# Reordering the head of a fused Fourier-mixing and expert kernel: which transfer stands ahead of which

## The chip, the cores and the metric

The kernel runs on one core of one Trainium2 chip. The metric is device time in microseconds (us) for one execution of the whole program. The kernel before was timed in three runs: 1634.4, 1637.09 and 1637.64 us, median 1637.09. A profiled execution of it took 1631.37 us, with a span of 1629.8 us in the trace; all times below that are given as positions ("at 201.6") are us from the start of that span.

## The reference

Two steps follow one another. The first mixes each sequence by a filter in the frequency domain, the second sends each of the resulting rows through one of eight small two-layer networks, chosen by a hash of the token number.

```python
# x: (8, 2496, 256) float32; filt_r, filt_i: (1249, 256)
X = np.fft.rfft(x, axis=1)
y = np.fft.irfft(X * (filt_r + 1j * filt_i)[None], n=2496, axis=1)   # (8, 2496, 256)

rows = y.reshape(19968, 256)
expert = token_ids * 2654435761 % 8                                # one of 8 per row
for e in range(8):                                                 # w1: (8, 256, 1024), w2: (8, 1024, 256)
    m = expert == e
    out[m] = np.maximum(rows[m] @ w1[e], 0.0) @ w2[e]
```

## The kernel before

The Fourier transform over 2496 = 39 x 64 points is done as three stages of matmuls per batch, with DRAM in between because each stage wants the data in another layout:

- **Stage 1** (six units per batch, tile `pa`): loads x in three parts (`load1`, v = 0, 1, 2), multiplies by `wf_t`, ScalarE copies the result out of PSUM and stores it to `d1` in DRAM.
- **Stage 2** (eleven units, tiles `pb`, `pc`): loads `t2` from `d1` in five parts (`load2`), multiplies by the table `d_t`; VectorE multiplies by the filter `f_t`; TensorE multiplies by the transposed table `e_t`; ScalarE copies the result and stores it to `d2`.
- **Stage 3** (six units, tile `pd`): loads `t4` from `d2` in three parts (`load4`), multiplies by `wi_t`, ScalarE copies into one of two buffers `o`, and GpSimd scatters the rows of `o`, up to four scatters for each unit, to their sorted places in `xs`.

The expert part then runs over 163 tiles of 128 sorted rows: load a tile `xg` from `xs`, transpose, two matmuls with a ReLU in between, scatter the rows to the output. The expert part can begin when batches 0 and 1 are through all three stages. What comes ahead of it is called the head here. The stages of batches 2 to 7 are woven into the expert tiles.

The order in which the head is emitted is given by hand: each piece has a number (its place in time), and the list is sorted by it. Every engine then works through its own instructions in that order, and the queues of SyncE, ScalarE and GpSimd issue their DMAs in that order. The numbers are places, not microseconds.

```python
    def load1(self, v):                      # x, in 3 DMAs on SyncE's queue
        k = self.b * NV + v
        if k < 4:                            # the first four parts lie in the weights' buffers
            xt = ws[k // 2][k % 2][0:NR]
            ...
        else:
            xt = xpool.tile([NR, XL, C], F32, ...)          # 2 buffers
        for h in range(H):
            nc.sync.dma_start(out=xt[h:NR:H, 0:n, :], in_=...)

    def load2(self, g):                      # t2: 4 buffers, 2 DMAs each on SyncE's queue
        ...
    def load4(self, v):                      # t4: 2 buffers, SyncE's queue
        ...
    def stage3(self, u):
        o = opool.tile([NR, XG, W], F32, ...)               # 2 buffers
        ...                                                 # VectorE writes the row numbers into o (line 288)
        self.products(wi_t, ..., o, copy, u, "pd")          # matmuls and copies
        for i in range(n):
            scatter(o[0:r, i, :], sidx[0:r, self.b, j:j + 1], f"xs_{self.b}")   # GpSimd

    def weights(i, which):                   # for i < 2: GpSimd's queue, 1 MB each
        eng = nc.gpsimd if i < 2 else nc.sync
        ...

    nc.sync.dma_start(out=wf_t[:], in_=wf_dram.ap())
    for v in range(NV):
        batches[0].load1(v)                  # x of batch 0
    ...
    S_PARTS = (slice(0, 8), slice(8, NS))    # tables and filters in two parts, NS = 20
    def load_tables(part):                   # d_t and both filters: GpSimd's queue, two DMAs on ScalarE's
        ...
    def spread_filters(part):                # sign and copy to the other 64 partitions
        ...
    def way_back(k):                         # e_t[4k:4k+4] from d_t by four transposes
        ...
    def count(): ...                         # VectorE and two small matmuls: rows of each expert
    def route(): ...                         # VectorE: the sorted place of each row
    def places():                            # the places to DRAM and back as indices sidx
        ...
        nc.gpsimd.dma_start(out=slot_dram[:]..., in_=slot_i[:])
        load_tables(1)
        ...                                  # three loads of sidx
    def blanks(): ...                        # seven scatters of empty rows into xs
```

Of the kernel before, what the change touches and what calls it, by code (L numbers as in the profile page):

```python
# [11 lines left out]
F32 = mybir.dt.float32  # L12
# [17 lines left out]
NS, NQ = N1 // 2 + 1, 64  # L30
# [6 lines left out]
NU = (HN + XG) // XG  # L37
# [75 lines left out]
def kernel(  # L113
# [10 lines left out]
    nc = tc.nc  # L124
# [3 lines left out]
    d_dram = nc.inline_tensor(d_host, name="d_tbl")  # L128
# [5 lines left out]
    def pool(stack, name, bufs, space=None):  # L134
        kw = {} if space is None else {"space": space}
        return stack.enter_context(tc.tile_pool(name=name, bufs=bufs, **kw))
# [23 lines left out]
    d_t = cpool.tile([P, NS, P], F32)  # L160
# [147 lines left out]
    batches = [Batch(b) for b in range(B)]  # L308
# [5 lines left out]
    def weights(i, which):  # L314

        if i >= NT:
            return
        if i >= 2 and which == 0:
            ws[i] = ws[i - 2]
        eng, kw = nc.gpsimd if i < 2 else nc.sync, {}  # L320
        e = eng.value_load(chunk_i[0:1, 0, i:i + 1], min_val=0, max_val=E - 1)
        if i >= 2:
            kw = {"cond": eng.value_load(chunk_i[0:1, 1, i:i + 1], min_val=0, max_val=1)}
        if which == 0:
            eng.dma_start(out=ws[i][0][:], in_=moe_w1[bass.ds(e, 1)].rearrange("one (dp p) f -> p (one dp) f", p=P), **kw)
        else:
            eng.dma_start(out=ws[i][1][:], in_=moe_w2[bass.ds(e, 1)].rearrange("one (fp p) d -> p (one fp) d", p=P), **kw)
# [3 lines left out]
    rpool = pool(rctx, "route", 1)  # L331
# [7 lines left out]
    nc.scalar.dma_start(out=rt[:], in_=r_dram.ap())  # L339
    nc.vector.tensor_copy(tokno[:], rt[0:NR, G + 2 + NQP:])  # L340

    S_PARTS = (slice(0, 8), slice(8, NS))

    def load_tables(part):
        sl = S_PARTS[part]
        nc.gpsimd.dma_start(out=d_t[:, sl, :], in_=d_dram.ap()[:, sl, :])
        for k in range(2):
            load_filter(k, sl)

    def load_filter(k, sl):  # L350
        filt = (filt_r, filt_i)[k]
        for q in range(2):
            off, step = (0, C) if q == 0 else (N1 * C, -C)
            (nc.gpsimd if k or sl.start else nc.scalar).dma_start(
                out=f_t[k][64 - 64 * k + 32 * q:96 - 64 * k + 32 * q, sl, :],
                in_=bass.AP(tensor=filt.tensor, offset=filt.offset + off + sl.start * step,
                            ap=[[N1 * C, 32], [step, sl.stop - sl.start], [1, C]]))

    def spread_filters(part):
        sl = S_PARTS[part]  # L360
        nc.vector.tensor_scalar(f_t[0][0:64, sl], f_t[0][64:128, sl], -1.0, None, op0=OP.mult)
        nc.scalar.copy(f_t[1][64:128, sl], f_t[1][0:64, sl])

    def way_back(k):

        ps = fps.tile([P, 4, P], F32, name=f"pe_{k}", tag="f")
        for i in range(4):
            nc.tensor.transpose(out=ps[:, i, :], in_=d_t[:, 4 * k + i, :], identity=ident[:])
        sl = slice(4 * k, 4 * k + 4)
        nc.scalar.activation(out=e_t[:, sl, :], in_=ps[:], func=AF.Identity, scale=sign[:])  # L370
# [102 lines left out]
    def places():  # L473
        slot, slot_i = rv["eid"], rv["eid_i"]
        nc.vector.tensor_reduce(slot[:], rv["acc"][:].rearrange("p e j -> p j e"), axis=AX.X, op=OP.add)
        nc.vector.tensor_copy(slot_i[:], slot[:])
        nc.gpsimd.dma_start(out=slot_dram[:].rearrange("(p j) -> p j", p=P), in_=slot_i[:])
        load_tables(1)
        for h in range(H):
            n = HN + (h == 0)  # L480
            slots = slot_dram[:]
            nc.gpsimd.dma_start(out=sidx[N1 * h:N1 * h + N1, :, 0:n],
                                in_=bass.AP(tensor=slots.tensor, offset=slots.offset + H0[h],
                                            ap=[[N2, N1], [S, B], [1, n]]))
# [62 lines left out]
    def spaced(t0, t1, n):  # L547
        return [t0 + (t1 - t0) * u / n for u in range(n)]

    def part1(b, at, loads=None):  # L550
        bt = batches[b]
        if loads is None:
            loads = [at[2 * v] - 2.5 * (at[1] - at[0]) for v in range(NV)]
        return ([(at[u], lambda u=u: bt.stage1(u)) for u in range(NU)] +
                [(loads[v], lambda v=v: bt.load1(v)) for v in range(NV) if b > 0])

    def part2(b, at, ready):
        bt = batches[b]
        return ([(at[u], lambda u=u: bt.stage2(u)) for u in range(NS // 2 + 1)] +
                [(max(at[2 * g] - 4.5 * (at[1] - at[0]), ready), lambda g=g: bt.load2(g)) for g in range(NS // SG)])  # L560

    def part3(b, at, ready):
        bt = batches[b]
        return ([(at[u], lambda u=u: bt.stage3(u)) for u in range(NU)] +
                [(max(at[2 * v] - 2.5 * (at[1] - at[0]), ready), lambda v=v: bt.load4(v)) for v in range(NV)])
# [4 lines left out]
    N_2 = NS // 2 + 1  # L570

    todo = part1(0, spaced(-153, -143, NU)) + [(-152.5, count), (-152.4, route)]
    todo += [(-154, lambda: load_tables(0)), (-129.5, places)]
    todo += [(t, lambda k=k: way_back(k)) for k, t in enumerate([-142.7, -142.5, -119.5, -119, -118.5])]
    todo += [(-129, lambda: spread_filters(0)), (-118.3, lambda: spread_filters(1))]
    todo += part2(0, spaced(-128, -95, N_2), -142)
    todo += part1(1, spaced(-123.5, -105, NU), [-141.5, -135, -134.5])
    todo += [(-125, tile_experts), (-121, experts), (-108, blanks)]  # L580
    todo += [(-110, lambda: nc.sync.dma_start(out=wi_t[:], in_=wi_dram.ap()))]
    todo += [(-118.2 + .1 * i, lambda i=i: (weights(i, 0), weights(i, 1))) for i in range(2)]
    todo += part2(1, spaced(-94, -60, N_2), -103) + part3(0, spaced(-84, -51, NU), -94.5)
    todo += part3(1, spaced(-54, -21, NU), -62) + part1(2, spaced(-52, -19, NU), [-85, -80, -41])

    todo += part1(3, spaced(2, 7, NU)) + part1(4, spaced(15, 20.5, NU))
    todo += part1(5, spaced(21, 27, NU)) + part1(6, spaced(36, 46, NU)) + part1(7, spaced(50, 60, NU))
# [109 lines left out]
```

## Time and profile before

The span splits into a head and the rest. From 207 on TensorE is almost always busy; up to 207 it is so for little more than half of the time.

| stretch (us) | what runs | TensorE busy (us) | granted clock | DMA share | GB/s |
|---|---|---|---|---|---|
| 0 to 42 | stage 1 of batch 0, tables, routing | 16.77 | 0.92 | 0.71 | 191 |
| 42 to 97 | stage 2 of batch 0, stage 1 of batch 1 | 38.32 | 0.81 | 0.97 | 308 |
| 97 to 148 | stage 2 of batch 1, stage 3 of batch 0 | 35.43 | 0.83 | 0.86 | 267 |
| 148 to 184 | stage 3 of batch 1, stage 1 of batch 2 | 24.55 | 0.83 | 0.70 | 203 |
| 184 to 207 | the turn to the expert part | 9.19 | 0.57 | 0.70 | 221 |
| 207 to 1630 | experts, batches 2 to 7 | 1394.54 | 1.00 | 0.47 | 146 |

How to read it: the busy time is how long the engine had an instruction at work in that stretch; the granted clock is the TensorE clock as a share of its full speed; the DMA share is the mean busy share of the core's 16 DMA engines. The queues are called q1 (SyncE), q10 (ScalarE) and q0 (GpSimd).

### The profile page before, as it was taken

How to read it: one execution, taken by the hardware profiler on the slowest of the kernel's cores; microseconds unless marked ns; L12 is line 12 of the kernel's file. 1: busy time of each engine (PE TensorE's matmuls, PEld its weight loads, DVE VectorE, ACT ScalarE, POOL GpSimd, SP SyncE). 2: the span in 40 equal slices, each digit the busy share in tenths (PEclk: the TensorE clock that was granted, in tenths of full speed). 3: DMA queues.
4: the chain of work that ended last, by engine and by line, in shares of the span. 5: the costliest groups of instructions: out<-in, count | busy, mean ns of one | idle time of the engine just before them, and what ended most of it. 6: DMA issues, size and time to landing. Idle time of an engine off the chain costs nothing.

```text
span 1629.8 us, 26685 instructions
## 1 busy us (share of the span) xinstructions
PE 1518.8 (93%) x9522; PEld 1381.7 (85%) x9522; DVE 539.0 (33%) x1022; ACT 217.1 (13%) x371; POOL 355.7 (22%) x375
## 2 busy tenths in 40 slices
PE   3676589999999999999999999999999999999997
PEld 2554378988888999899989998999999999999997
DVE  6572142452244444233434442222122121221221
ACT  2322212112111111111111111000000000000000
POOL 0235300331320132122121322233111111111111
PEclk9788699999999999999999999999999999999999
DMA  7998627747864883674537643544152413132220
GB/s 189 306 290 244 198 98 205 240 165 207 245 218 150 244 256 111 194 197 147 185 114 222 199 135 115 147 127 162 45 203 79 140 37 126 52 94 88 84 84 9
DMA packets 152541, 258.77 MB, mean 159 GB/s; under 512 B 16185, under 2 KB 118508, under 8 KB 150410
## 3 DMA queue, kind: packets, MB, share of 16 engines
q1 hardware_dynamic: 103345, 163.46, 33.1%
q0 software_dynamic: 21136, 50.96, 9.4%
q10 hardware_dynamic: 27928, 42.65, 8.3%
q8 instruction: 76, 1.25, 0.3%
q14 instruction: 56, 0.45, 0.1%
HBM read 431.87 MB, written 86.09 MB: 318 GB/s over the span
## 4 chain that ended last, share of the span: by engine, by line
PE 42%; issue 36%; POOL 7%; DMA 3%; DVE 2%; POOLq 1%; ACT 0%; SPq 0%; ACTq 0%; DVEq 0%
PE ups L630 15%; PE dps L642 15%; POOL out_dram L646 6%; PE pb L240 3%; PE pa L203 3%; PE pc L263 3%; PE pd L203 2%; POOL xs L301 2%; DMA xs<-o,sidx 1%; PE xps L619 1%; DVE z L250 1%; PE pa L198 0%; POOLq L646 0%; DMA d<-g 0%; DVE y L247 0%
## 5 line engine op out<-in xcount | busy, mean ns | idle before, releaser
L630 PEld LDWEIGHTS ups<-xt,w 128*128 128x128 f32 x5216 | 610.3, 193 | 9.2 <-DVE xt L621 1.0
L630 PE MATMUL ups<-xt,w 128*128 128x128 f32 x5216 | 611.1, 276 | 0.6 <-DVE xt L621 0.6
L642 PE MATMUL dps<-w,ht 128*128 128x256 f32 x2608 | 591.0, 380 | 0.0
L642 PEld LDWEIGHTS dps<-w,ht 128*128 128x128 f32 x2608 | 490.0, 191 | 63.7 <-issue 1.6
L646 POOL DMA_INDIRECT out_dram<-osb,xg x163 | 159.6, 979 | 944.6 <-DVE osb L645 919.4
L636 DVE TENSOR_SCALAR ht<-ups 128x512 f32<-128x512 f32 x163 | 112.8, 692 | 526.8 <-PE ups L630 519.7
L634 ACT ACTIVATE ht<-ups 128x512 f32<-128x512 f32 x163 | 97.3, 597 | 1008.0 <-PE ups L630 992.3
L301 POOL DMA_INDIRECT xs<-o,sidx x176 | 175.3, 996 | 245.7 <-DVE o L205 145.7
L645 DVE COPY osb<-dps 128x256 f32<-128x256 f32 x163 | 69.3, 425 | 404.5 <-PE dps L642 396.2
L240 PE MATMUL pb<-t,d_t 128*128 128x256 f32 x320 | 91.1, 413 | 23.8 <-DMA t<-d 23.3
L250 DVE TENSOR_TENSOR z<-pb,filt 64x512 f32<-64x512 f32 x160 | 110.1, 688 | 2.2
L263 PE MATMUL pc<-y,e_t 128*128 128x256 f32 x320 | 90.1, 407 | 19.7 <-DVE y L251 19.3
L240 PEld LDWEIGHTS pb<-t,d_t 128*128 128x128 f32 x320 | 63.5, 209 | 35.5 <-issue 25.9
L263 PEld LDWEIGHTS pc<-y,e_t 128*128 128x128 f32 x320 | 63.3, 203 | 35.8 <-issue 17.5
L203 PE MATMUL pd<-t,wi_t 120*117 120x256 f32 x320 | 81.2, 399 | 11.7 <-DMA t<-d 7.1
L203 PEld LDWEIGHTS pd<-t,wi_t 120*117 120x117 f32 x320 | 58.9, 191 | 25.5 <-issue 9.1
L247 DVE TENSOR_TENSOR y<-pb,filt 128x512 f32<-128x512 f32 x80 | 55.3, 691 | 68.3 <-PE pb L240 67.8
L266 ACT COPY g<-pc 128x512 f32<-128x512 f32 x80 | 46.8, 585 | 233.2 <-PE pc L263 229.8
L621 DVE COPY xt<-xps 128x256 f32<-128x256 f32 x163 | 67.6, 415 | 1.9 <-PE xps L619 1.9
L619 PE MATMUL xps<-ident,xg 128*128 128x128 f32 x326 | 62.6, 274 | 3.1 <-DMA xg<-xs 3.1
L203 PE MATMUL pa<-x,wf_t 117*120 117x256 f32 x264 | 63.3, 383 | 0.6 <-DVE z L250 0.6
L205 ACT COPY t<-pa 120x512 f32<-120x512 f32 x80 | 46.0, 588 | 90.6 <-PE pa L203 88.1
(102 smaller groups left out, 352.5 us busy)
## 6 DMA issues: line engine op xcount, KB each, us to landing
w<-in_moe_w_dram SPq DMA_DIRECT2D x322, 1024.0 KB
xg<-xs SPq DMA_DIRECT2D x163, 136.0 KB
t<-d SPq DMA_DIRECT2D x80, 256.0 KB
d<-g ACTq DMA_DIRECT2D x80, 256.0 KB
d<-t ACTq DMA_DIRECT2D x16, 960.0 KB
t<-d SPq DMA_DIRECT2D x16, 960.0 KB
x<-in_x_dram SPq DMA_DIRECT2D x39, 312.0 KB
x<-in_x_dram SPq DMA_DIRECT2D x21, 234.0 KB
```

Source lines behind the costliest of these rows:

```text
L203: nc.tensor.matmul(out=ps[0:cols * H, k, :], lhsT=w[:], rhs=src[:, 2 * i + k, :], start=True, stop=True)
L240: nc.tensor.matmul(out=ps[:, i, :], lhsT=d_t[:, s, :], rhs=self.t2[s // SG][:, s % SG, :], start=True, stop=True)
L250: nc.vector.tensor_tensor(out=z[b], in0=ps[a], in1=f_t[1][a, sl, :], op=OP.mult)
L263: nc.tensor.matmul(out=ps[:, i, :], lhsT=e_t[:, 2 * u + i, :], rhs=pr[:, i, :], start=True, stop=True)
L301: st = nc.gpsimd.indirect_dma_start(out=xs[:], out_offset=bass.IndirectOffsetOnAxis(ap=index, axis=0), in_=rows, in_offset=None, bounds_ch ...
L619: nc.tensor.transpose(out=ps[:, dp, :], in_=xg[i][:, dp * P:(dp + 1) * P], identity=ident[:])
L630: nc.tensor.matmul(out=ps[:, k, :], lhsT=w1[:, dp, fp * P:(fp + 1) * P], rhs=xt[i][:, dp, :], start=(dp == 0), stop=(dp == DP - 1))
L634: nc.scalar.activation(out=dst, in_=ps[:], func=AF.Relu)
L636: nc.vector.tensor_scalar_max(dst, ps[:], 0.0)
L642: nc.tensor.matmul(out=ps[:], lhsT=ht[:, fp, :], rhs=w2[:, fp, :], start=(fp == 0), stop=(fp == FP - 1))
L645: nc.vector.tensor_copy(out=o[:], in_=ps[:])
L646: st = nc.gpsimd.indirect_dma_start(out=out[:], out_offset=bass.IndirectOffsetOnAxis(ap=xg[i][:, C:C + 1].bitcast(I32), axis=0), in_=o[:], ...
```

## The change

The numbers of the head's pieces change, and with them the order of its transfers. The aim is that each transfer comes in the order in which its data is needed:

- The tables and filters come in three parts instead of two. The first is issued on SyncE's queue behind x of batch 0; before, it was issued on the two other queues beside it.
- The second and third part are issued on GpSimd's queue, each behind a small GpSimd copy that reads one element of a tile and so waits for it: the second part behind the last part of x of batch 0, the third behind the first `t2` of batch 0.
- `places` comes right behind `route`, and no longer issues tables.
- The three loads of x of batch 1 come later, between the loads of stage 2 of batch 0; stage 1 of batch 1 too comes later against stage 2 of batch 0.
- The first weights, four DMAs of 1 MB, leave their place beside stage 2 of batch 0, and come after the second and the third unit of stage 3 of batch 0.
- Stage 3 of batch 0 is packed closer against stage 2 of batch 1. Some small pieces move along.

```diff
-    S_PARTS = (slice(0, 8), slice(8, NS))
+    S_PARTS = (slice(0, 8), slice(8, 12), slice(12, NS))
+    junk = rpool.tile([1, 1], F32)
+
+    def behind(ap):
+        nc.gpsimd.tensor_copy(junk[:], ap)
 
     def load_tables(part):
         sl = S_PARTS[part]
-        nc.gpsimd.dma_start(out=d_t[:, sl, :], in_=d_dram.ap()[:, sl, :])
+        eng = nc.gpsimd if part else nc.sync
+        eng.dma_start(out=d_t[:, sl, :], in_=d_dram.ap()[:, sl, :])
         for k in range(2):
-            load_filter(k, sl)
+            load_filter(k, sl, eng)
 ...
-            (nc.gpsimd if k or sl.start else nc.scalar).dma_start(
+            eng.dma_start(
 ...                                          (in places)
-        load_tables(1)
 ...
-    todo = part1(0, spaced(-153, -143, NU)) + [(-152.5, count), (-152.4, route)]
-    todo += [(-154, lambda: load_tables(0)), (-129.5, places)]
-    todo += [(t, ... way_back(k)) for k, t in enumerate([-142.7, -142.5, -119.5, -119, -118.5])]
-    todo += [(-129, lambda: spread_filters(0)), (-118.3, lambda: spread_filters(1))]
-    todo += part2(0, spaced(-128, -95, N_2), -142)
-    todo += part1(1, spaced(-123.5, -105, NU), [-141.5, -135, -134.5])
-    todo += [(-125, tile_experts), (-121, experts), (-108, blanks)]
+    first = batches[0]
+    todo = part1(0, spaced(-155, -143, NU)) + [(-152.5, count), (-152.4, route), (-152.3, places)]
+    todo += [(-154.9, lambda: load_tables(0)), (-152.45, lambda: behind(first.x[2][0:1, 0, 0:1]))]
+    todo += [(-152.44, lambda: load_tables(1))]
+    todo += [(-129, lambda: behind(first.t2[0][0:1, 0, 0:1])), (-128.9, lambda: load_tables(2))]
+    todo += [(t, ... way_back(k)) for k, t in enumerate([-142.7, -142.5, -120, -109, -108.8])]
+    todo += [(-141, lambda: spread_filters(0)), (-117.5, lambda: spread_filters(1)), (-111.5, lambda: spread_filters(2))]
+    todo += part2(0, spaced(-127, -97, N_2), -138) + part1(1, spaced(-117, -102, NU), [-133, -131, -128])
+    todo += [(-140, tile_experts), (-125, experts), (-100, blanks)]
     todo += [(-110, lambda: nc.sync.dma_start(out=wi_t[:], in_=wi_dram.ap()))]
-    todo += [(-118.2 + .1 * i, lambda i=i: (weights(i, 0), weights(i, 1))) for i in range(2)]
-    todo += part2(1, spaced(-94, -60, N_2), -103) + part3(0, spaced(-84, -51, NU), -94.5)
-    todo += part3(1, spaced(-54, -21, NU), -62) + part1(2, spaced(-52, -19, NU), [-85, -80, -41])
+    todo += part2(1, spaced(-94, -60, N_2), -101) + part3(0, spaced(-84, -58, NU), -94.5)
+    todo += [(-79 + 6 * i, lambda i=i: (weights(i, 0), weights(i, 1))) for i in range(2)]
+    todo += part3(1, spaced(-54, -21, NU), -58) + part1(2, spaced(-52, -19, NU), [-85, -80, -50])
```

(Cuts are marked with `...`. `part1`, `part2` and `part3` give the units of a stage their places; the last argument of `part1` holds the places of its three loads of x, that of `part2` and `part3` the earliest place of a load from DRAM.)

More of the change, by code (lines that the diff above doesn't have):

```diff
@@ L340, with load_filter @@
     nc.vector.tensor_copy(tokno[:], rt[0:NR, G + 2 + NQP:])
-    S_PARTS = (slice(0, 8), slice(8, NS))
+    S_PARTS = (slice(0, 8), slice(8, 12), slice(12, NS))
+    junk = rpool.tile([1, 1], F32)
+    def behind(ap):
+        nc.gpsimd.tensor_copy(junk[:], ap)
     def load_tables(part):
         sl = S_PARTS[part]
-        nc.gpsimd.dma_start(out=d_t[:, sl, :], in_=d_dram.ap()[:, sl, :])
+        eng = nc.gpsimd if part else nc.sync
+        eng.dma_start(out=d_t[:, sl, :], in_=d_dram.ap()[:, sl, :])
         for k in range(2):
-            load_filter(k, sl)
-    def load_filter(k, sl):
+            load_filter(k, sl, eng)
+    def load_filter(k, sl, eng):
         filt = (filt_r, filt_i)[k]
@@ L570 @@
     N_2 = NS // 2 + 1
-    todo = part1(0, spaced(-153, -143, NU)) + [(-152.5, count), (-152.4, route)]
-    todo += [(-154, lambda: load_tables(0)), (-129.5, places)]
-    todo += [(t, lambda k=k: way_back(k)) for k, t in enumerate([-142.7, -142.5, -119.5, -119, -118.5])]
-    todo += [(-129, lambda: spread_filters(0)), (-118.3, lambda: spread_filters(1))]
-    todo += part2(0, spaced(-128, -95, N_2), -142)
-    todo += part1(1, spaced(-123.5, -105, NU), [-141.5, -135, -134.5])
-    todo += [(-125, tile_experts), (-121, experts), (-108, blanks)]
+    first = batches[0]
[3 more added lines that the diff above has]
+    todo += [(-129, lambda: behind(first.t2[0][0:1, 0, 0:1])), (-128.9, lambda: load_tables(2))]
+    todo += [(t, lambda k=k: way_back(k)) for k, t in enumerate([-142.7, -142.5, -120, -109, -108.8])]
+    todo += [(-141, lambda: spread_filters(0)), (-117.5, lambda: spread_filters(1)), (-111.5, lambda: spread_filters(2))]
+    todo += part2(0, spaced(-127, -97, N_2), -138) + part1(1, spaced(-117, -102, NU), [-133, -131, -128])
+    todo += [(-140, tile_experts), (-125, experts), (-100, blanks)]
     todo += [(-110, lambda: nc.sync.dma_start(out=wi_t[:], in_=wi_dram.ap()))]
-    todo += [(-118.2 + .1 * i, lambda i=i: (weights(i, 0), weights(i, 1))) for i in range(2)]
-    todo += part2(1, spaced(-94, -60, N_2), -103) + part3(0, spaced(-84, -51, NU), -94.5)
-    todo += part3(1, spaced(-54, -21, NU), -62) + part1(2, spaced(-52, -19, NU), [-85, -80, -41])
+    todo += part2(1, spaced(-94, -60, N_2), -101) + part3(0, spaced(-84, -58, NU), -94.5)
+    todo += [(-79 + 6 * i, lambda i=i: (weights(i, 0), weights(i, 1))) for i in range(2)]
+    todo += part3(1, spaced(-54, -21, NU), -58) + part1(2, spaced(-52, -19, NU), [-85, -80, -50])
     todo += part1(3, spaced(2, 7, NU)) + part1(4, spaced(15, 20.5, NU))
```

## The prediction

> **What bounds the kernel now.** I first cut the span into stretches (the table of windows), to see where TensorE, which is busy 93% of the span, isn't.
>
> ```profile
> 0.00:207.00 207.00, 124.25 (x430) 91.67 (x430) 98.81 (x197) 53.22 (x90) 64.56 (x80) 0.82 0.82 246
> 207.00:1630.00 1423.00, 1394.54 (x9093) 1290.04 (x9092) 440.24 (x825) 163.90 (x281) 291.13 (x295) 1.00 0.47 146
> ```
>
> The columns after the stretch's length are busy us of TensorE, its weight loads, VectorE, ScalarE and GpSimd, then clock, DMA share and GB/s. From 207 on TensorE is busy for 1394.5 of 1423 us: nothing but less TensorE work shortens that, and the change takes none away. So the whole effect is by how much the first expert tile moves from where it now starts, 206.4. The chain of waits, in order of time, tells what leads up to it:
>
> ```profile
> 162.35 7.05 DMA xs<-o,sidx
> ...
> 174.58 5.51 DMA xs<-o,sidx
> ...
> 185.16 4.27 DMA d<-t
> ...
> 190.54 3.18 DMA t<-d
> ...
> 201.63 4.66 DMA xg<-xs
> 206.43 0.68 PE xps L619 x2
> ```
>
> Stage 3 of batch 1 runs at the pace of its scatters into two buffers; then SyncE's queue, in order, waits for batch 2's stage 1 to reach DRAM, loads its `t2` (ten DMAs from 189.98) and three parts of x, and only at 201.6 issues the first `xg`. The change leaves this tail, 148 to 206.4, in the same order. I call the start of stage 3 of batch 1 (now 148.0) T; the first tile then comes some 58 us after T. What sets T is in the same table of windows:
>
> ```profile
> 0.00:42.00 42.00, 16.77 (x58) 13.04 (x59) 26.66 (x72) 10.84 (x16) 3.51 (x15) 0.92 0.71 191
> 42.00:97.00 55.00, 38.32 (x137) 28.55 (x136) 33.93 (x62) 16.47 (x25) 17.19 (x22) 0.81 0.97 308
> 97.00:148.00 51.00, 35.43 (x129) 26.26 (x127) 28.62 (x46) 12.74 (x23) 21.85 (x23) 0.83 0.86 267
> 148.00:184.00 36.00, 24.55 (x88) 17.64 (x88) 1.32 (x6) 11.63 (x23) 22.02 (x23) 0.83 0.70 203
> ```
>
> Between 42 and 97 no engine is busy two thirds of the time except TensorE at reduced clock, while the DMA engines are at 0.97: this stretch is bound by bytes in flight. 97 to 148 is nearly so (0.86). 0 to 42 is not: TensorE's timeline shows it idle at both ends.
>
> ```profile
> 15.73 3.74 PE L203 MATMUL pa<-w,wf_t 117*120 117x256 f32 x8 [15.73 <-DMA w<-in_x_dram]
> ...
> 41.04 3.75 PE L240 MATMUL pb<-t,d_t 128*128 128x256 f32 x8 [7.30 <-DMA t<-d]
> ...
> 71.01 2.05 PE L240 MATMUL pb<-t,d_t 128*128 128x256 f32 x4 [6.48 <-DMA t<-d]
> ...
> 147.98 3.45 PE L203 MATMUL pd<-t,wi_t 120*117 120x256 f32 x8 [3.86 <-DMA t<-d]
> ```
>
> It waits 15.7 us for the first x (which shares the engines with tables), 7.3 us for the first `t2`, and at 71.0 for a `t2` that was issued at 53.8 and took 17 us among tables, x of batch 1 and 4 MB of weights.
>
> [...] The trace before has no scatter behind weights. [...] x is loaded by 39 rows at a time, and from 16 to 20, when x is nearly all there is, the share is 0.81 and 0.79[...]. So x alone won't fill the engines.
>
> **The change, part by part.**
>
> *Start of stage 1.* x of batch 0 is 2.56 MB, tokens 0.16, the first tables 1.57 (d_t 0.52, four filter DMAs of 0.26): 4.3 MB by about 20.5. [...] SyncE's queue has moved 3.65 MB at a share of 29.8% of 42 us, that is 292 GB/s for 16 engines[...]. The first part of x (0.96 MB) needs 4 us, from about 2.5 us on[...]: 7.5 instead of 15.7. All of x is in by about 14. Stage 1's 44 matmuls (x8, x32 and twice x2 in the timeline) took from 15.7 to 32.7, 17 us; from 7.5 that ends at 24.5.
>
> *First t2.* Gained 8 us, but not all lasts. After 14 us there remain 1.57 MB of first tables, 0.79 MB of the new second part and 2.6 MB of d1: 4.96 MB at some 260 GB/s (214 to 231 GB/s were moved at a share of 0.85 between 25 and 35), 19 us: d1 has landed at 33, not 37. VectorE agrees: routing starts when the counting matmuls are done (19.5 now; behind two units now, so about 15), then 21.4 us of `route` and `places` (20.2 to 41.5 now), then 1.2 us for the filters' sign: ready at 38 instead of 42.7. Stage 2 starts **4 us** earlier.
>
> *Stage 2 of batch 0.* 55 us at 308 GB/s are 16.9 MB. Out of it go the weights (4.2 MB) and the second part of the tables (0.8): 11.9 MB, 39 us at the same rate, **16 us** less. VectorE's floor is ten units of 2.8 us (0.69 + 1.39 + 0.69), 28 us, and doesn't bind. The tables that units 4 and 5 need are already there, so TensorE's wait at 56.2 (3.05 us for d_t) goes too.
>
> *Stage 2 of batch 1 and stage 3 of batch 0.* 51 us at 267 GB/s are 13.6 MB; the weights add 4.2: 17.8 MB, at the full rate of 308 GB/s 58 us, **7 us** more. On GpSimd, four weight issues (0.73 to 1.39 us each, now at 56.7 to 67.2) come among the scatters, 22 a batch at 1.3 us each (0.99 + 0.30), 29 us in all: room enough in 58 us.
>
> *Stage 3 of batch 1.* Now the first unit's copies wait until 152.2 for a buffer that unit 4 of batch 0 still scatters from. With stage 3 of batch 0 packed in beside stage 2, this wait should go: up to **4 us**, of which I take 2.
>
> *Added elsewhere.* Two GpSimd copies of one element: well under 1 us, nothing waits for GpSimd there. SyncE's queue gets five more issues, at 0.5 to 0.75 us each, off the path.
>
> Sum: -4 - 16 + 7 - 2 = -15 us if bytes alone bind. I take 4 us off for what the weights do to the scatters (next part): -11 us, **1626 us**.
>
> **Rivals.**
>
> *Weights turn stage 3 of batch 0 into the new bound.* A pair is 2.1 MB; at GpSimd's share of the DMA time between 56 and 75 (53% of 319 GB/s, 170 GB/s) it takes 12 us. Scatters issued behind it land after some 12 us instead of 6.4 (the median from issue to landing at 113 to 125), and with two `o` buffers ScalarE's next copies wait; ScalarE also carries stage 2's copies, and TensorE is in order, so stage 2 of batch 1 stalls too. Two pairs, each 6 us: 12 us. For it: VectorE now waits 45.2 us in nine waits for scatters to release `o`. Against it: in bytes this is the 7 us already counted, and these two overlap. At worst T stays at 148 or goes a little beyond: 1637 to 1640.
>
> *Bytes only move.* From 42 to 148 the engines are nearly full, and all bytes must be through before T. Then only idle DMA time can be won: 0.03 x 55 + 0.14 x 51 = 9 us at most, and the 0.8 MB fetched earlier, 2.6 us. That is at most 12 us, and more likely half: 1626 to 1632. It is nearly the sum above by another way, and caps it.
>
> *Stage 3 or VectorE sets T anyway.* Both stages 2 need 56 us of VectorE; from 39 on that ends at 95 at best, and T is 148. Much slack, so this doesn't bind; if bytes flowed better (large weight rows moved at 400 GB/s near 70 to 75) T could fall to 130: 1619.
>
> **Range and chances.** The centre is 1626, between the second rival's ends and the sum. Below, 1616 would take both a T of about 130 and some of stage 3's wait; above, 1638 is the weights rival in full. The 2% limits are 1604.3 and 1669.8; the first needs 33 us out of a head whose idle DMA time up to 207 is 0.18 x 207 = 37 us, some of it in the untouched tail: hardly. The second needs a long stall at each pair of weights.
>
> **What would show it.** Right: the first `pa` near 7.5; the first `pb` near 37 to 39; last `pc` of batch 0 near 80; the first `pd` near 90; T at 135 to 141; the first `xps` 56 to 58 us after T, and the rest after it as long as now, 1423 us. Wrong: scatters landing in over 12 us behind the weights with ScalarE waiting on them, and T at 148 or later; or `t2` loads of batch 0 late behind x of batch 1 in SyncE's own queue, so that the last `pc` isn't before 90. The prediction fails altogether if the tail after T changes, or if the expert part itself runs into waits at its start because of later weights.

## The result, and the profile after

The changed kernel takes 1646.57 us (median of 4 runs, 1644.32 to 1650.61) against 1637.37 us for the kernel before beside it: a ratio of 1.0063, with a 95% interval of 1.0037 to 1.0089. It is slower by some 10 us, where the prediction had it 11 us faster.

The table of windows of the changed kernel, cut where the first expert tile starts, at 215.8 (columns as before):

```profile
0.00:216.00 216.00, 118.33 (x430) 86.19 (x430) 98.97 (x198) 53.98 (x91) 66.47 (x84) 0.80 0.79 235
216.00:1640.00 1424.00, 1398.65 (x9094) 1291.19 (x9092) 440.26 (x825) 163.96 (x281) 291.34 (x295) 0.99 0.47 146
```

As foreseen, the expert part is what it was, and the difference lies in the head: the first tile comes 9.4 us later (206.4 to 215.8), and the medians are 9.2 us apart. In this one profile the rest takes 3.5 us longer as well (1426.9 against 1423.4 us); between 430 and 530 the granted clock is 0.97 where it was 1.00. The thirteen versions profiled later, on several chips, have a rest of 1424 to 1433 us whether their ratio is high or low, so I don't count it to the change.

The same stretches of the head as before:

```profile
0.00:42.00 42.00, 18.81 (x67) 13.51 (x68) 30.48 (x81) 10.96 (x16) 7.22 (x21) 0.80 0.80 234
42.00:97.00 55.00, 37.00 (x146) 26.94 (x145) 35.07 (x62) 17.54 (x28) 10.89 (x16) 0.91 0.79 233
97.00:148.00 51.00, 26.63 (x106) 20.34 (x106) 24.17 (x40) 10.74 (x19) 24.79 (x24) 0.87 0.89 286
148.00:184.00 36.00, 18.15 (x69) 13.94 (x70) 0.78 (x4) 9.76 (x18) 15.87 (x17) 0.74 0.72 189
```

The first stretch moves more bytes, as meant (234 GB/s against 191). But in the second the DMA share has fallen from 0.97 to 0.79, and the rate from 308 to 233 GB/s: with the weights gone, the engines are simply less busy. In the third, TensorE has lost 8.8 us of work (26.63 against 35.43 us). TensorE's timeline tells where:

```profile
8.15 5.27 PE L203 MATMUL pa<-w,wf_t 117*120 117x256 f32 x16 [8.15 <-DMA w<-in_x_dram]
...
37.75 2.04 PE L240 MATMUL pb<-t,d_t 128*128 128x256 f32 x4 [6.54 <-DMA t<-d]
...
85.23 1.13 PE L263 MATMUL pc<-y,e_t 128*128 128x256 f32 x4 [2.05 <-DVE y L251]
...
102.56 1.96 PE L203 MATMUL pd<-t,wi_t 120*117 120x256 f32 x8 [0.86 <-DMA t<-d]
...
137.40 3.73 PE L203 MATMUL pd<-t,wi_t 120*117 120x256 f32 x8 [15.11 <-DMA t<-d]
140.93 1.10 PE L240 MATMUL pb<-t,d_t 128*128 128x256 f32 x4
...
157.61 3.73 PE L203 MATMUL pd<-t,wi_t 120*117 120x256 f32 x8 [7.91 <-DMA t<-d]
```

Every step is early until 121: stage 1 by 7.6 us, stage 2 by 3.3, the first `pd` (102.56, line 203) by 8.6. Then TensorE stands 15.1 us for the `t4` of unit 4 of batch 0's stage 3. Behind it, in TensorE's order, stand the last two units of stage 2 of batch 1 (the `pb` at 140.93), which could have followed at 122. In the kernel before, that unit also ran at 138.0, but behind stage 2's end. Its timeline, from the last `pc` of batch 0 (96.42) and of batch 1 (134.18) to unit 4:

```profile
96.42 2.05 PE L263 MATMUL pc<-y,e_t 128*128 128x256 f32 x4 [1.81 <-DVE y L251]
...
134.18 1.10 PE L263 MATMUL pc<-y,e_t 128*128 128x256 f32 x4 [2.14 <-DVE y L251]
138.00 3.73 PE L203 MATMUL pd<-t,wi_t 120*117 120x256 f32 x8 [2.73 <-DMA t<-d]
```

So T, the start of stage 3 of batch 1, went from 148.0 to 157.6.

The chain of waits shows the same, with what held the `t4`:

```profile
113.60 5.38 DMA d<-g
118.99 0.74 SPq L186
...
119.84 17.43 DMA t<-d
...
137.40 3.73 PE pd L203 x8
...
149.94 7.53 DMA t<-d
...
157.61 3.73 PE pd L203 x8
```

SyncE's queue waits for a store that ScalarE issued (`d<-g`, batch 1's), then issues x of batch 2, then the `t4`, which needs 17.4 us to land: four weights of 1 MB were issued at 115.4 to 124.3, and the first two took a median of 16.1 us from issue to landing.

### The profile page after: what moved, and what is told of

It is laid out like the page before. It is cut to its first block, busy times and chain, and to the rows that moved or that the text cites. A ratio compares the mean times of both kernels' runs of the same rounds, so it can differ in the third digit from the quotient of the medians.

```text
span 1642.7 us, 26690 instructions
## 1 busy us (share of the span) xinstructions
PE 1517.0 (92%) x9522; PEld 1377.4 (84%) x9522; DVE 539.2 (33%) x1023; ACT 217.9 (13%) x372; POOL 357.8 (22%) x379
## 4 chain that ended last, share of the span: by engine, by line
issue 44%; PE 34%; POOL 9%; DMA 8%; DVE 2%; ACT 1%; POOLq 1%; SPq 1%; ACTq 0%; DVEq 0%
PE ups L637 11%; PE dps L649 11%; POOL out_dram L653 6%; PE pa L203 3%; POOL xs L301 3%; PE pb L240 2%; DMA t<-d 2%; PE pc L263 2%; PE pd L203 2%; DMA d<-t 2%; DMA d<-g 1%; DMA xs<-o,sidx 1%; DVE z L250 1%; DMA xg<-xs 1%; PE xps L626 1%
## 5 line engine op out<-in xcount | busy, mean ns | idle before, releaser
L649 PEld LDWEIGHTS dps<-w,ht 128*128 128x128 f32 x2608 | 491.3, 191 | 66.2 <-issue 2.0
L263 PE MATMUL pc<-y,e_t 128*128 128x256 f32 x320 | 86.4, 394 | 19.7 <-DVE y L251 18.9
L203 PEld LDWEIGHTS pa<-x,wf_t 117*120 117x120 f32 x264 | 48.8, 190 | 11.2 <-ACT t L205 1.2
```

The costliest lines, as they stand in the source:

```text
L203: nc.tensor.matmul(out=ps[0:cols * H, k, :], lhsT=w[:], rhs=src[:, 2 * i + k, :], start=True, stop=True)
L263: nc.tensor.matmul(out=ps[:, i, :], lhsT=e_t[:, 2 * u + i, :], rhs=pr[:, i, :], start=True, stop=True)
L649: nc.tensor.matmul(out=ps[:], lhsT=ht[:, fp, :], rhs=w2[:, fp, :], start=(fp == 0), stop=(fp == FP - 1))
```

## The experiments

Two theories stood. **A**, order: unit 4 now stands ahead of stage 2's last units, so its late `t4` blocks them. **B**, bytes: the weights fill the DMA engines in the stretch that sets T, wherever they stand. Each kernel was timed against the kernel before on the same chip, in five rounds; the ratios below are to that kernel, whose median was 1635.65 to 1645.65 us from group to group. To compare, the change as it is has 1.0063. T and other positions come from one profiled execution each, on different chips, and that of the kernel before (1631.4 us) lies below its median; a few us of T between groups should not be read as an effect, and the ratios are the firmer measure.

**Late units back behind stage 2.** On the changed kernel:

```diff
-part3(0, spaced(-84, -58, NU), -94.5)
+part3(0, spaced(-84, -58, NU)[:4] + [-62, -56.5], -94.5)
```

> The changed kernel with the last two units of batch 0's stage 3 put back behind the last unit of batch 1's stage 2 in the engines' order (places -62 and -56.5, as before); all transfers keep the changed order. Theory A (the late t4 of batch 0 blocks TensorE, and with it the last two units of stage 2): those units run near 122 to 128 instead of 141 to 146, T falls from 157.6 to 145-149, the first expert tile from 215.8 to 204-207, time 1633-1638. Theory B (the DMA engines are full with the moved weights until about 138, and T waits for bytes, not for order): T stays at 153 or later, time 1642-1647.

Measured: ratio 1.0002 (0.9987 to 1.0017), T at 150.5, first tile at 209.6. The whole loss is gone, though T misses A's range by 1.5 us and the first tile by 2.6. But the head's earlier start has not arrived either.

**The third x of batch 2 back to its place**, on the changed kernel and together with the edit above:

```diff
-part1(2, spaced(-52, -19, NU), [-85, -80, -50])
+part1(2, spaced(-52, -19, NU), [-85, -80, -41])
```

> The changed kernel with the third x load of batch 2 back at its old place, behind the last t4 load of batch 1 on SyncE's queue. Theory A says T stays at 157-158, but the wait of 9.3 us for that t4 (issued at 171.1 because the x load ahead of it waits for a buffer) goes; scatters then run on without the gap at 176-181: the first expert tile 4-6 us earlier, near 211, time 1640-1643. If instead the scatters' two buffers set the pace of stage 3 of batch 1 anyway, nothing changes: 1645-1647.

> Both of the former edits on the changed kernel. If the two waits are separate, their gains add: T 145-149 and a tail of 52-55 instead of 58 us, first expert tile 198-203, time 1628-1634, faster than the kernel before. If the weights among the scatters are what costs (theory B), time stays above 1638.

Measured: 1.0043 (1.0028 to 1.0058) alone, which overlaps the change's own interval; 1.0005 (0.9991 to 1.002) with both, the same as without this edit. A miss: that wait of TensorE is worth nothing that these runs can tell. Alone, the first tile came at 223.1 in its profile, not near 211, as T was 164.9: unit 4 there waited 19.1 us for its `t4`. In the profile of both together the first tile came 63.9 us after T, not less than 58: TensorE then waited up to 5.6 us for ScalarE's copies into `o` instead.

**Weights early again**, on the changed kernel, right behind the second unit of batch 1's stage 1:

```diff
-(-79 + 6 * i, lambda i=i: (weights(i, 0), weights(i, 1)))
+(-114.4 + .1 * i, lambda i=i: (weights(i, 0), weights(i, 1)))
```

> The changed kernel with the first weights issued beside stage 2 of batch 0 again (right behind the second unit of batch 1's stage 1), all else as changed. Theory A and B both say that the t4 of batch 0 (issued at 119.8, landing at 137.3 among 4.2 MB of weights) lands by 128, so T falls to 147-150 and the time to 1635-1639, if stage 2 of batch 0 gives no more than 2-3 us back; the DMA share of 60 to 85, now near 0.7, has room for the weights. If stage 2 of batch 0 were bound by bytes as the prediction held, it would end 10 us or more later and the time would stay at 1644-1648.

Measured: 1.0011 (0.9994 to 1.0028), so most of the loss goes by this edit too; but T was 154.7 in its profile, outside what I expected, and the first tile at 213.0. Stage 2 of batch 0 gave back more than 2 to 3 us. TensorE waited 7.1 us for a `t2` at 72.5, in a stretch (42 to 97) that moved 269 GB/s, against 233 in the changed kernel, and the last `pc` came at 92.58:

```profile
72.51 2.04 PE L240 MATMUL pb<-t,d_t 128*128 128x256 f32 x4 [7.13 <-DMA t<-d]
...
92.58 1.32 PE L263 MATMUL pc<-y,e_t 128*128 128x256 f32 x4 [2.05 <-DVE y L251]
```

Without weights beside it, the changed kernel has this `pc` at 85.2, and the version with the late units, from the same chip as this one, at 87.3. So in the changed order the weights' bytes cost stage 2 some 5 to 7 us.

**Both edits together**, the late units and the weights early:

> The changed kernel with both edits that each won back most of the loss: the last two units of batch 0's stage 3 behind stage 2 of batch 1, and the first weights early again. What stays of the change: the head's tables in three parts, x of batch 0 first, x of batch 1 between stage 2's loads, the closer packing of the first four units. Theory A (order and weights work through one and the same wait, the late t4 of batch 0): the gains don't add, ratio to the kernel before 0.996-1.001, T 147-150. Theory B (they cost separately): the gains add, ratio 0.990-0.995, T 140 or earlier.

Measured: 0.9998 (0.9988 to 1.0007), T at 147.9. The gains don't add, as A expected: either edit undoes the wait at unit 4. But this alone doesn't clear the weights. Beside stage 2 they cost there (the last `pc` of batch 0 came at 93.0), which may hide what they no longer cost among the scatters.

**Weights last**, behind all of stage 3, with the late units back:

```diff
-(-79 + 6 * i, lambda i=i: (weights(i, 0), weights(i, 1)))
+(-20 + .1 * i, lambda i=i: (weights(i, 0), weights(i, 1)))
```

> The changed kernel with the late units put back, and the first weights issued only after all of stage 3 of batch 1. Then neither stage 2 nor stage 3 shares the DMA engines with 4.2 MB of weights. If bytes set T (theory B), T falls to 138-143, and the ratio to 0.992-0.998, unless the weights themselves, issued near 180 and landing near 205, hold up the first tile. If T is set by the chain of dependent steps and not by bytes, T is at 146-150 as with the late units alone, and the ratio 0.999-1.004.

Measured: 1.001 (0.9999 to 1.002). T fell to 144.4, between the two ranges, and 3.5 us ahead of the version before, from the same chip, with the weights beside stage 2: B has a share. But the gain was given back later: the `t2` of batch 2, among the weights, took 12.6 us to land instead of 3.2, and the first tile came at 212.9.

**Each part alone, on the kernel before.** First the packing:

```diff
-part3(0, spaced(-84, -51, NU), -94.5)
+part3(0, spaced(-84, -58, NU), -94.5)
```

> The kernel before with one part of the change alone: stage 3 of batch 0 packed closer, so that its unit 4 stands ahead of the last two units of batch 1's stage 2 in TensorE's order. Theory A: unit 4's t4 lands near 138 as before, now with units 9 and 10 of stage 2 blocked behind it; these end at 145 instead of 134, T 155-158, ratio 1.005-1.007: the whole loss of the change by this part alone. Theory B: no more than 3 us, ratio up to 1.002.

Measured: 1.0054 (1.0041 to 1.0067), +8.8 us on 1637. Its chain of waits:

```profile
122.97 8.23 DMA d<-g
131.27 5.17 DMA t<-d
136.58 3.73 PE pd L203 x8
...
157.13 3.73 PE pd L203 x8
```

T at 157.1 and a span of 1642.8 us: the changed kernel's numbers, with no weights moved. (The closer places also move units 1 and 3 by one unit of stage 2; the first experiment, which put back units 4 and 5 alone, ties the loss to these.) By the chain, the `t4` is issued as late as 131.27 because SyncE's queue waits 8.2 us for the landing of a store of ScalarE, and this store belongs to batch 1, while the `t4` reads batch 0's rows, long since written. That a queue is held by another queue's completion that its data doesn't need is what the chain shows; I have no run that takes such a wait away by itself.

Then the weights alone:

```diff
-(-118.2 + .1 * i, lambda i=i: (weights(i, 0), weights(i, 1)))
+(-78 + 5.5 * i, lambda i=i: (weights(i, 0), weights(i, 1)))
```

> The kernel before with the other part alone: the first weights moved behind the second and third unit of batch 0's stage 3. Stage 2 of batch 0 should end 3-8 us earlier (no weights beside it), then stage 3 of batch 0 has scatters that land after 12-14 us instead of 6.4. Theory A: units 4 and 5 stand behind stage 2 here, so little of it reaches T: ratio 0.997-1.002. Theory B (bytes, or the scatters' buffers, cost by themselves): T 152 or later, ratio 1.003-1.006.

Measured: 1.0031 (1.0018 to 1.0045), +5.1 us, T at 151.0, unit 4 after a wait of 10.1 us at 142.9. A expected too little here; the weights cost by themselves. And stage 2 of batch 0, now without them, ended only 1.3 us earlier (last `pc` at 95.1 against 96.4), not 3 to 8.

**How the weights cost.** To see this I moved the `t4` of unit 4 ahead of x of batch 2 in SyncE's queue, and left the rest of the change alone:

```diff
-part1(2, spaced(-52, -19, NU), [-85, -80, -50])
+part1(2, spaced(-52, -19, NU), [-85, -74, -50])
```

> The changed kernel with one load moved: the second x of batch 2 (three DMAs) goes behind the last t4 load of batch 0 on SyncE's queue, instead of ahead of it. The order on TensorE, the packing and the weights stay as changed. Theory A (TensorE stands at unit 4 until its t4 has landed, and stage 2's last units stand behind it): t4 is issued near 113 instead of 119.8, lands near 125 to 131 instead of 137.3, and T falls by as much, to 147-152: ratio to the kernel before 1.000-1.004. If the position of unit 4 matters in some other way than through this t4, nothing moves: 1.005-1.007.

Measured: 1.0036 (1.0024 to 1.0049), within the range; T at 153.8, 1.8 us above its range. The `t4` was now issued at 114.9 and unit 4 ran at 122.4, after a wait of 0.6 us: the first knot is gone, and a second appears, in ScalarE's timeline (copies of stage 2, `g`, and of stage 3, `o`):

```profile
121.78 1.07 ACT L205 COPY o<-pd 117x512 f32<-117x512 f32 x2 [3.63 <-DMA xs<-o,sidx]
122.74 0.60 ACT L266 COPY g<-pc 128x512 f32<-128x512 f32 x1
123.38 1.11 ACTq L270 DMA_DIRECT2D d<-g  x2
135.21 1.07 ACT L205 COPY o<-pd 117x512 f32<-117x512 f32 x2 [11.87 <-DMA xs<-o,sidx]
136.17 0.60 ACT L266 COPY g<-pc 128x512 f32<-128x512 f32 x1
```

ScalarE waits 11.9 us for a scatter to release an `o` buffer, and stage 2's last copies wait behind it. VectorE stands at the same scatters, for it writes the row numbers into `o` (line 288), and by VectorE the wait reaches TensorE, whose last `pc` needs a `y` that stands behind that write:

```profile
135.62 0.39 DVE L288 TENSOR_SCALAR o<-tokno 117x64 int32<-117x64 f32 x1 [10.76 <-DMA xs<-o,sidx]
```

```profile
139.00 2.05 PE L263 MATMUL pc<-y,e_t 128*128 128x256 f32 x4 [12.87 <-DVE y L251]
```

The scatters stand behind the weights in GpSimd's queue. The time from issue to landing of the scatters, first at 110 to 125 in the kernel before, then at 115 to 127 in the changed kernel, behind the weights:

```profile
DMA to landing us min/median/max: 5.0/6.4/6.7
```

```profile
DMA to landing us min/median/max: 11.8/13.3/14.7
```

This is the rival of the prediction with its number: 12 us instead of 6.4 was estimated, 13.3 measured. The traces show the longer time to landing, not by what mechanism; with the weights on SyncE's queue, in a later run below, the median was 6.4 us.

**What the head's part is worth.** The tables' part alone on the kernel before: x of batch 0 first, tables in three parts, `places` behind `route`.

> The kernel before with the first part of the change alone: x of batch 0 first, tables in three parts, places behind route; x and stage 1 of batch 1, weights and stage 3 stay at their places of before. The prediction's step says stage 2 of batch 0 starts 4 us earlier (at 37-39). If that gain is carried through, T is at 143-145 and the ratio 0.997-0.998. If it is spent on waits in stage 2 of batch 0, which shares the DMA engines with tables, x and weights as before, T is at 147-149 and the ratio 0.999-1.001.

Measured: 0.9971 (0.9957 to 0.9984), -4.7 us on 1637: by the ratio this part keeps its gain. T was 146.5, in neither range, and the first tile at 204.6, only 1.8 us earlier than in the profile before; the two traces alone would not show 4.7 us.

With batch 1's x and stage 1 in the changed order on top, and the weights right behind its second unit:

> The kernel before with the tables' part of the change and, on top, x and stage 1 of batch 1 in the changed order (later, between stage 2's loads); the first weights stand right behind the second unit of that stage 1, stage 3 as before. The tables alone gave 0.997, the same with this order and four units packed closer 1.000. If the later x of batch 1 is what takes those 4 us (stage 2 of batch 1 can't start before batch 1's stage 1 is in DRAM), the ratio is 0.999-1.002 and the first t2 of batch 1 is issued at 92 or later, against 88.7 with the tables alone. If it is the closer packing of the four units, the ratio stays at 0.996-0.998.

Measured: 0.999 (0.9975 to 1.0005); the first `t2` of batch 1 was issued at 95.2, not 88.7. T was 150.2, and the first tile at 207.2. The later x seems to take some of the gain back, but the two intervals overlap, and the weights stand later too. This isn't settled.

With the tables alone and the weights out of stage 2, on SyncE's queue behind the last x of batch 2 (`-40`, `eng = nc.sync`):

> The tables' part of the change alone, with the first weights on SyncE's queue behind the last x of batch 2. If the weights' bytes beside stage 2 of batch 0 cost time, T falls below the 146.5 of the tables alone, to 141-144, and the ratio to 0.993-0.996. If stage 2 of batch 0 is set by its chain of loads and not by bytes, T stays at 145-147, and the ratio at 0.997-1.000, the weights now slowing the scatters of batch 1 by up to 5 us.

Measured: 0.9971 (0.996 to 0.9983). The stretch of stage 2 in the tables of windows, first with the tables alone, then with the weights taken out:

```profile
42.00:97.00 55.00, 35.13 (x141) 26.33 (x140) 31.70 (x57) 16.96 (x27) 6.34 (x11) 0.84 0.93 289
```

```profile
42.00:97.00 55.00, 37.19 (x142) 27.27 (x141) 32.68 (x58) 16.95 (x27) 6.81 (x13) 0.83 0.76 221
```

The DMA share falls from 0.93 to 0.76, 68 GB/s less for 55 us; the last `pc` of batch 0 comes at 92.3 instead of 94.7, and T goes from 146.5 to 146.15: next to nothing. In this order the last six x loads of batch 1 stand together ahead of `t2` loads in SyncE's queue, and TensorE still waits 9.1 us for such a `t2` at 66.4 (11.2 us with the weights). The share of 0.93 did not mean that bytes alone set the length. But the weights cost nothing here only because something else held stage 2. Its length, from the first `pb` to the last `pc` of batch 0, in the profiles:

| x and stage 1 of batch 1 | weights beside stage 2 (us) | weights elsewhere (us) |
|---|---|---|
| order of before | 55.4, 55.7 | 54.3, 53.3 |
| changed order | 54.9, 54.0, 54.4 | 47.5, 49.0, 50.2, 47.2 |

(In the first row: the kernel before and the tables alone; the weights alone moved, and this run. In the second: the weights early, both edits together, and the tables with x of batch 1; the change, the late units, the weights last, and the last version below. The other versions in the changed order, with the weights elsewhere, have 46.6 to 48.6.) The later x alone shortens stage 2 by about 1 us, the weights taken out alone by 1 to 2, both together by 4 to 8.

This run also bears on queue against bytes for the scatters. While its weights move on SyncE's queue, at 337 GB/s in all from 160 to 185 (333 from 115 to 125 in the changed kernel), the scatters of batch 1 issued at 164 to 185 take:

```profile
DMA to landing us min/median/max: 2.9/6.4/8.4
```

That is a median of 6.4 us (4.8 in the same window of the kernel before), against 13.3 behind the weights in GpSimd's own queue.

**A version that beats both.** The changed kernel with the late units back, and the weights on SyncE's queue behind the last `t4` of batch 1, where that queue issues nothing more until 189.4 in this version's profile:

```diff
-(-79 + 6 * i, lambda i=i: (weights(i, 0), weights(i, 1)))
+(-45 + .1 * i, lambda i=i: (weights(i, 0), weights(i, 1)))
...
-part3(0, spaced(-84, -58, NU), -94.5)
+part3(0, spaced(-84, -58, NU)[:4] + [-62, -56.5], -94.5)
...
-eng, kw = nc.gpsimd if i < 2 else nc.sync, {}
+eng, kw = nc.sync, {}
```

> The changed kernel with the late units put back behind stage 2 of batch 1, and the first weights on SyncE's queue behind the last loads of stage 3 of batch 1, where that queue has nothing else until 186 and the DMA share is 0.65. So the weights stand neither in stage 2, nor ahead of scatters in their queue, nor in the turn to the expert part. If weights in the way were all that kept the head's gain from arriving, T is at 143-146, the first expert tile at 201-204 and the ratio 0.996-0.999, better than both kernels. If the weights slow the scatters by bytes alone, T is at 143-146 but the tail grows from 58 to 61-64 us: ratio 0.999-1.002.

Measured: 0.9961 (0.9945 to 0.9976), the lowest ratio of all, though not apart from the tables alone. Four versions with the late units differ in nothing but the place and queue of the weights: beside stage 2 0.9998, among the scatters 1.0002, behind stage 3 1.001, and here 0.9961, with its interval below the other three. In TensorE's timeline:

```profile
142.31 3.45 PE L203 MATMUL pd<-t,wi_t 120*117 120x256 f32 x8 [9.65 <-DMA t<-d]
...
205.60 0.66 PE L626 MATMUL xps<-ident,xg 128*128 128x128 f32 x2 [3.33 <-DMA xg<-xs]
```

T is the earliest of all, 142.3. The tables alone, from the same chip, had 146.5. But the tail is 63.3 us instead of 58.1 there, so the 4 us gained at T are not seen at the first tile. The engines now carry scatters and weights at once (from 160 to 190, SyncE's queue took 49.0% of the 16 engines' time and GpSimd's 17.9%); that this is what lengthens the tail is likely, not shown.

## Why the prediction was wrong, step by step

- **What bounds the kernel: right.** The effect is the shift of the first tile, and the tail from T to it was called 58 us; it is 58.4 before and 58.2 after. All hung on T.
- **Start of stage 1 (7.5) and of stage 2 (37 to 39): right**, 8.15 and 37.75, 3.3 of the 4 us in this profile. The 4 us for the first part of x were my estimate (0.96 MB at 0.81 of 292 GB/s); with the 2.5 us ahead of them they give 6.5; what is left up to 7.5 no trace had shown. Measured, it is 6.7 us from the first issue of x, at 1.42, to the first `pa`. The two GpSimd copies took 0.18 and 0.36 us, and SyncE's five further issues were over at 15.4. By the ratio the earlier starts reach the end when the tables' part stands alone (-4.7 us). That the x load alone leaves some engines idle also held: from 3 to 8 in the changed kernel, with little but x on the way, the share is 0.78.
- **Stage 2 of batch 0, "16 us less": the step that failed first; half of the size.** It took a DMA share of 0.97 for a proof that bytes alone set the length, and kept 308 GB/s with 5 MB less to move. Measured: the rate fell to 233 GB/s, and stage 2 became 7.9 us shorter (55.4 to 47.5); the last `pc` came at 85.2 (96.4 before), where the list of signs had 80, and the sum itself 96.4 - 20 = 76. What the bytes left free, waits in a chain of steps took up. In the changed kernel SyncE's queue, for one, spends 44.1 to 58.5 on three x loads of batch 1, 12.0 us of it waiting for a store of ScalarE, and the next `t2` loads are issued only at 58.5. I had named x of batch 1 in SyncE's queue as a danger, but given it no time.
- **From the last `pc` of batch 0 to T: the step that turned the sign.** The sum had this stretch 7 us longer for the weights and 2 shorter for the packing, or 9 longer with the 4 us for the scatters. By the profiles it grew from 51.6 to 72.4 us, by 20.8. Two terms were wrong:
- **Stage 2 of batch 1 and stage 3 of batch 0, "7 us more": mechanism incomplete.** In the prediction's terms moving the weights was worth some 13 of the 16 us in stage 2, less these 7 and the 4 for the scatters: -2 us. Alone it measured +5.1 us: stage 2 of batch 0 won only 1.3 us by it, and the `t4` and the scatters do come late.
- **Packing, "this wait should go": the sign was wrong.** I counted only a buffer wait of up to 4 us in stage 3 of batch 1, and didn't see which unit came to stand ahead of which in TensorE's order. By the places of the change, unit 4 went from -62 to -66.7, past the last two units of stage 2 at -66.2 and -63.1. Its `t4` landed at 138 in the profile before; that one line was enough to see that stage 2 would stop there. It costs 8.8 us alone.
- **The rivals.** The first, weights and scatters, did occur, with the landing time that was given, but was held to at most 1640. The second, "bytes only move", shared the premise that bytes alone set the pace. None spoke of a unit placed ahead of others on TensorE whose data comes late.

By the ratios the single parts are tables -4.7, weights +5.1, packing +8.8, together +9.2 us; the change is +10.3 (6 to 15). That they add up so well is partly chance: packing and weights meet at the same `t4`, taking back either one was nearly enough, and the weights' cost in stage 2 depends on the order of x. What x of batch 1 in its later place costs, some 3 us by two ratios with overlapping intervals, stays open.

## What to carry to other kernels

A stretch with busy DMA engines is not yet one that bytes alone set: ask what the freed time would be filled with, and try taking bytes out before counting on the rate. Here taking them out won 1 to 2 us in one order of the other loads, and 4 to 8 in another. When instructions are packed closer on an engine that works in order, write down for each moved one when its data lands now, and what comes to stand behind it; here unit 4 cost little at the end of a stage (a wait of 2.7 us at 138.0 in the kernel before), and most of its wait in front of another's last units (15.1 us in the changed kernel, with T 9.6 us later). In this kernel bulk loads did best on a queue that had nothing urgent behind them: the same weights cost time beside stage 2, ahead of scatters and among the next stage's loads (0.9998 to 1.001), and least in a gap of SyncE's queue (0.9961).

## What was unexpected of the hardware

The queues of SyncE and ScalarE are not independent in this program: SyncE's loads waited up to 12.0 us, by what the trace gives as the releaser, for the landing of stores that ScalarE had issued and whose data they did not read. And a gain in the middle of the head is easily lost: with the weights last, T was 3.6 us ahead of the kernel before, and the time was at a ratio of 1.001.
